# Silu MLP on one core: the last output group in row halves instead of whole rows

## The chip, the core and the metric

The kernel runs on one core of a Trainium2 chip. The metric is device time in microseconds (us) for one launch. Engines are named as the profile names them: PE is TensorE (PEld its weight loads), ACT is ScalarE, DVE is VectorE, POOL is GpSimd, and SP is SyncE, which here only starts DMAs. SPq and ACTq are the DMA issues of SP and of ACT.

## The reference

```python
def reference(x, w1, w2):
    h = jnp.einsum("bsd,df->bsf", x, w1)
    h = _silu(h)
    out = jnp.einsum("bsf,fd->bsd", h, w2)
    return out
```

All arrays are bfloat16: x is 1 x 2048 x 640 (2048 tokens), w1 is 640 x 1728, w2 is 1728 x 640 and the output is 1 x 2048 x 640.

## The kernel before

The tokens are cut into four chunks of 512 (`NSC`). The hidden dimension of 1728 is 13 tiles of 128 (`FT`) and a rest of 64 (`FL`). The output dimension of 640 is split in columns 0 to 511 (`DA`) and 512 to 639.

The first matmul produces h transposed, hidden rows on partitions, with ScalarE's silu writing it to `hT` (and the rest of 64 rows to `hTt`, two chunks sharing its 128 partitions). The second matmul then has two forms. `Wide(c)` computes columns 512 to 639 for a chunk, transposed, and a DMA transpose turns them into `o_sb`. `Tok(st, a, e)` computes columns a to e of the 128 tokens of block `st`, with `hT` as the stationary operand and `w2s` as the moving one, into one PSUM bank of 512 fp32 columns.

Most of the second matmul is in groups of four units (`quad`). In it each 128-row step is cut in two halves of 64 rows. `half` issues one such matmul; two units in two banks are interleaved by `lanes`, one of them on rows 0 to 63 and the other on rows 64 to 127, so that two half matmuls can run at the same time. `begin` issues a unit's 13 halves on one side and the tail, which is the rest of 64 hidden rows; `rest` issues the 13 halves on the other side. A unit's first phase and its second phase write the same bank from different rows, so `rest` is preceded by a wait for the end of the first phase (`halfway`).

The last group is written out differently: five units, A, B and C of 512 columns and the fourth token block as E of 384 and G2 of 128 columns. The five tails come first, then each unit's 13 matmuls over whole rows of 128 (`whole`), unit by unit.

`close` casts a unit from PSUM to `o_sb` (`evac`, line 254 on DVE or 256 on ACT) and issues a store (line 88). A store through SP carries the columns 512 to 639 along when the unit ends at column 512, so that a row has 640 columns. Only G2's store goes through ACT's DMA queue. The order on each engine is the order in the program. At the end SP waits for all of its stores and ACT for its own.

Every matmul of this stage has the profile line 175 (`mm`) and every load or store the line 88 (`load`), so groups are told apart by operands and time.

Of the kernel before, what the change touches and what calls it, by code (L numbers as in the profile page):

```python
# [9 lines left out]
def bass_standalone__dense_activation_silu__prompt_kernel(  # L10
# [10 lines left out]
    of = out.flatten_outer_dims()  # L21
    S, D = xf.shape
    F = w1.shape[1]
    P = 128
# [3 lines left out]
    FT = F // P  # L28
    FL = F - FT * P
# [4 lines left out]
    DA = 512  # L34
# [4 lines left out]
    pe, act, dve, pool, sp = nc.tensor, nc.scalar, nc.vector, nc.gpsimd, nc.sync  # L39

    with ExitStack() as es:
        def sb(name, shape, dtype):
            return es.enter_context(nc.sbuf_tensor(name, shape, dtype))
# [3 lines left out]
        w2s = sb("w2s", [P, FT, D], bf16)  # L47
        w2t = sb("w2t", [P, D], bf16)
        hT = sb("hT", [P, FT, S], bf16)
        hTt = sb("hTt", [P, NSC // 2, SCH], bf16)  # L50
        oT = sb("oT", [P, S], bf16)
        o_sb = sb("o_sb", [P, S // P, D], bf16)
        warm = sb("warm", [P, 32], fp32)
        z = sb("z", [P, HB], bf16)
        ps = es.enter_context(nc.psum_tensor("ps", [P, NB, BANK], fp32))
# [4 lines left out]
        def sem(name):  # L60
            s = es.enter_context(nc.semaphore(name))
            count[s.name if hasattr(s, "name") else name] = 0
            return [s, 0]

        def tick(ins, s, n=1):
            ins.then_inc(s[0], n)
            s[1] += n
            return (s, s[1])

        def wait(eng, *points):  # L70
            for pt in points:
                if pt is None:
                    continue
                s, v = pt
                key = (id(eng), id(s))
                if seen.get(key, 0) < v:
                    eng.wait_ge(s[0], v)
                    seen[key] = v

        s_pe, s_act, s_dve = sem("s_pe"), sem("s_act"), sem("s_dve")  # L80
# [4 lines left out]
        def load(eng, out_ap, in_ap):  # L85
            s = sem(f"s_ld{n_dma[0]}")
            n_dma[0] += 1
            return tick(eng.dma_start(out=out_ap, in_=in_ap), s, 16)
# [85 lines left out]
        def mm(o, l, r, start, stop, shared=False):  # L174
            return pe.matmul(o, lhsT=l, rhs=r, start=start, stop=stop, skip_group_check=shared)  # L175
# [7 lines left out]
        def step(b, k, ft, c0, c1, start=False, stop=False):  # L183
            for h0 in (0, HC):
                ins = mm(ps[h0:h0 + HC, b, :], w1s[:, k, ft * P + h0:ft * P + h0 + HC],
                         xT[:, k, c0:c1], start, stop, shared=True)
            return ins

        def part(k, ft, c0, c1, start=False, stop=False):
            return step(ft, k, ft, c0, c1, start, stop)  # L190
# [18 lines left out]
        for ft in range(NO):  # L209
            t = tick(part(4, ft, 0, SCH, stop=True), s_pe)  # L210
# [11 lines left out]
        for ft in range(NO, FT):  # L222
# [3 lines left out]
            for k in range(DT):  # L226
                ins = step(b, k, ft, 0, SCH, start=(k == 0), stop=(k == DT - 1))
            silu(hT[:, ft, 0:SCH], ps[:, b, :], b, tick(ins, s_pe))
        for c in range(1, NSC):
            wait(pe, ld_xc[c])  # L230
            for ft in range(FT):
                b = bank()
                for k in range(DT):
                    ins = step(b, k, ft, c * SCH, (c + 1) * SCH, start=(k == 0), stop=(k == DT - 1))
                h_last = silu(hT[:, ft, c * SCH:(c + 1) * SCH], ps[:, b, :], b, tick(ins, s_pe))
        h_tail = []
        for q in range(NSC // 2):
            b = bank()
            for k in range(DT):
                for hh in range(2):  # L240
                    c = 2 * q + hh
                    ins = mm(ps[hh * FL:(hh + 1) * FL, b, :], w1s[:, k, F0:F],
                             xT[:, k, c * SCH:(c + 1) * SCH],
                             start=(k == 0), stop=(k == DT - 1), shared=True)
# [4 lines left out]
        def evac(out_ap, in_ap, b, after, eng=None):  # L249
            e = eng or (dve, act)[evac_n[0] % 2]  # L250
            evac_n[0] += 1
            wait(e, after)
            if e is dve:
                r = tick(dve.tensor_copy(out=out_ap, in_=in_ap), s_dve)  # L254
            else:
                r = tick(act.copy(out=out_ap, in_=in_ap), s_act)  # L256
            bank_free[b] = r
            return r

        JB = SCH // P  # L260
        HP = P // 2
        stores, stores_a = [], []
        s_turn = [sem(f"s_turn{c}") for c in range(NSC)]
        st_w = [None] * NSC

        class Wide:
# [11 lines left out]
            def tail(self):  # L278
                q, r0 = self.c // 2, (self.c % 2) * FL
                return mm(ps[:, self.b, :], w2t[r0:r0 + FL, DA:D], hTt[r0:r0 + FL, q, :],  # L280
                          False, False, shared=True)

            def close(self, t):
                c = self.c
                r = evac(oT[:, c * SCH:(c + 1) * SCH], ps[:, self.b, :], self.b, t)
                wait(sp, r)
                st_w[c] = tick(sp.dma_start_transpose(
                    out=o_sb[:, c * JB:(c + 1) * JB, DA:D],
                    in_=oT[:, c * SCH:(c + 1) * SCH],
                ), s_turn[c], 16)  # L290

        class Tok:
# [8 lines left out]
                return mm(ps[:, self.b, 0:self.e - self.a], hT[r0:r0 + HP, ft, st * P:(st + 1) * P],  # L301
                          w2s[r0:r0 + HP, ft, self.a:self.e], start, stop, shared=True)

            def whole(self, ft, stop):
                st = self.st
                return mm(ps[:, self.b, 0:self.e - self.a], hT[:, ft, st * P:(st + 1) * P],
                          w2s[:, ft, self.a:self.e], False, stop, shared=True)

            def tail(self, start=False):
                st = self.st  # L310
                c = st // JB
                q, r0, col = c // 2, (c % 2) * FL, (st % JB) * P
                return mm(ps[:, self.b, 0:self.e - self.a], hTt[r0:r0 + FL, q, col:col + P],
                          w2t[r0:r0 + FL, self.a:self.e], start, False, shared=True)

            def close(self, t, eng=None):
                st, a, e = self.st, self.a, self.e
                r = evac(o_sb[:, st, a:e], ps[:, self.b, 0:e - a], self.b, t, eng)
                last = a > 0
                if e == DA and not last:  # L320
                    e = D
                q = act if last else sp
                wait(q, r, st_w[st // JB])
                (stores_a if last else stores).append(
                    load(q, of[st * P:(st + 1) * P, a:e], o_sb[:, st, a:e]))

        def lanes(up, down):
            for i in range(max(len(up), len(down))):
                for lane in (up, down):
                    if i < len(lane):  # L330
                        lane[i]()

        def begin(u, r0):
            def end():
                wait(pe, *h_tail)
                u.halfway = tick(u.tail(), s_pe)
            return [lambda ft=ft: u.half(r0, ft, ft == 0, False) for ft in range(FT)] + [end]

        def rest(u, r0, done):
            ops = [lambda ft=ft: u.half(r0, ft, False, ft == FT - 1) for ft in range(FT - 1)]  # L340
            ops.append(lambda: done.append(tick(u.half(r0, FT - 1, False, True), s_pe)))
            return ops
# [18 lines left out]
        last = None  # L361
        for q in range(NSC // 2):
            for j in range(0, JB, 2):
                s0, s1 = 2 * q * JB + j, (2 * q + 1) * JB + j
                if q < NSC // 2 - 1 or j < JB - 2:
                    quad(Tok(s0), Tok(s1), Tok(s0 + 1), Tok(s1 + 1))
                else:
                    last = (s0, s1)
        s0, s1 = last
        A, B, C, E, G2 = Tok(s0), Tok(s1), Tok(s0 + 1), Tok(s1 + 1, 0, 384), Tok(s1 + 1, 384, DA)  # L370
        wait(sp, st_w[(s1 + 1) // JB])
        stores.append(load(sp, of[(s1 + 1) * P:(s1 + 2) * P, DA:D], o_sb[:, s1 + 1, DA:D]))
        for u in (A, B, C, E, G2):
            u.open()
        wait(pe, *h_tail)
        for u in (A, B, C, E, G2):
            u.tail(start=True)
        for u, eng in ((A, dve), (B, act), (C, act), (E, dve), (G2, act)):
            for ft in range(FT):
                ins = u.whole(ft, ft == FT - 1)  # L380
            u.close(tick(ins, s_pe), eng)
        wait(sp, *stores)
        wait(act, *stores_a)

# [27 lines left out]
```

## Time and profile before

| | us |
|---|---|
| Median of 3 runs | 124.34 (124.25 to 124.39) |
| Profiled execution | 124.57 |
| Its span | 123.1 |
| PE busy | 120.7 (98%) |
| ACT busy | 38.8 (32%) |
| DVE busy | 6.9 (6%) |
| Last quad and the last group, until the last cast starts | 98.0 to 121.27 |
| From the last cast to the span's end | 1.8 |

The granted TensorE clock is full (1.0) from 5 us to the last matmul. Matmul records overlap: the duration of one (for example 0.376 us for 64 rows by 512 columns) includes the latency through the array, and the rate is read from the distance between starts. A DMA issue on SPq or ACTq is the time for which the issuing engine is occupied; the landing of the data comes later (a median of 1.8 us from issue for SP's output stores of 160 KB). A few matmul records may be missing.

### The profile page before, as it was taken

Reading aid. Unit: us, or ns where it says so; the run is one execution under the profiler, and the core shown is the slowest. Engines: PE = TensorE matmul, PEld = TensorE weight load, DVE = VectorE, ACT = ScalarE, POOL = GpSimd, SP = SyncE. Lnnn points to the kernel's source line nnn. Section 1 sums busy time; section 2 is a strip of 40 time slices with the busy share of each in tenths; the row PEclk is TensorE's granted clock in tenths of the full one; section 3 lists DMA queues with packets and bytes.
Section 4 is the critical chain, followed back from the end, with each engine's and each line's share of the span. In section 5 each row is a group of like instructions: output and inputs, shape, how many; then the busy total and the mean of one; then the engine's idle time right before and its main releaser. Section 6 shows DMA issues by size and latency. Waiting matters only on the chain.

```text
span 123.1 us, 2300 instructions
## 1 busy us (share of the span) xinstructions
PE 120.7 (98%) x1056; PEld 59.5 (48%) x1057; DVE 6.9 (6%) x11; ACT 38.8 (32%) x67; POOL 0.3 (0%) x5
## 2 busy tenths in 40 slices
PE   8999999999999999999999999999999999999993
PEld 5455555555555555555544444444444444444452
DVE  0000000000000000000000022002201300222001
ACT  4002975555555555555530011001101200110110
POOL 0000000000000000000000000000000000000000
PEclk9999999999999999999999999999999999999999
DMA  6999935555992000000000004202200220023112
GB/s 146 263 248 315 135 86 108 104 87 92 280 392 77 0 0 0 8 0 0 0 0 5 0 12 113 51 0 107 107 0 5 107 107 0 5 107 117 53 67 83
DMA packets 19625, 10.42 MB, mean 85 GB/s; under 512 B 13728, under 2 KB 19104, under 8 KB 19616
## 3 DMA queue, kind: packets, MB, share of 16 engines
q1 hardware_dynamic: 19328, 10.08, 31.0%
q10 hardware_dynamic: 288, 0.20, 0.6%
q8 instruction: 8, 0.13, 0.5%
q14 instruction: 1, 0.01, 0.0%
HBM read 4.51 MB, written 2.62 MB: 58 GB/s over the span
## 4 chain that ended last, share of the span: by engine, by line
PE 98%; issue 0%; ACT 0%; DVEq 0%
PE ps L175 95%; PE ps L132 3%; ACT o_sb L256 0%; DVEq L397 0%
## 5 line engine op out<-in xcount | busy, mean ns | idle before, releaser
L175 PE MATMUL ps<-xT,w1s 128*64 128x512 bf16 x540 | 59.2, 382 | 0.0
L175 PE MATMUL ps<-w2s,hT 64*128 64x512 bf16 (+3 forms) x376 | 46.0, 369 | 0.2 <-issue 0.2
L175 PEld LDWEIGHTS ps<-xT,w1s 128*64 128x64 bf16 x540 | 30.6, 111 | 28.3 <-issue 0.9
L179 ACT ACTIVATE hT<-ps 128x512 bf16<-128x512 f32 x52 | 30.0, 608 | 29.2 <-PE ps L175 29.2
L175 PEld LDWEIGHTS ps<-w2s,hT 64*128 64x128 bf16 (+1 forms) x377 | 21.0, 95 | 24.1 <-issue 0.2
L256 ACT CAST o_sb<-ps 128x512 bf16<-128x512 f32 (+1 forms) x9 | 4.9, 550 | 41.5 <-PE ps L175 41.5
L175 PE MATMUL ps<-hT,w2s 64*128 64x512 bf16 x104 | 11.7, 376 | 0.0
L175 PEld LDWEIGHTS ps<-hT,w2s 64*128 64x128 bf16 x104 | 5.0, 94 | 6.3 <-issue 0.4
L254 DVE CAST o_sb<-ps 128x512 bf16<-128x512 f32 (+1 forms) x8 | 5.4, 675 | 40.5 <-PE ps L175 40.5
L254 DVE CAST oT<-ps 128x512 bf16<-128x512 f32 x2 | 1.4, 691 | 73.5 <-PE ps L175 73.5
L256 ACT CAST oT<-ps 128x512 bf16<-128x512 f32 x2 | 1.2, 585 | 10.6 <-PE ps L175 10.6
L132 PE MATMUL ps<-z 128*128 128x256 bf16 (+1 forms) x15 | 3.3, 419 | 0.4 <-DVE z L125 0.4
L175 PE MATMUL ps<-w2t,hTt 64*128 64x512 bf16 (+2 forms) x17 | 2.9, 363 | 0.0
L132 PEld LDWEIGHTS ps<-z 128*128 128x128 bf16 (+1 forms) x15 | 1.9, 143 | 1.5 <-issue 0.4
L179 ACT ACTIVATE hTt<-ps 128x512 bf16<-128x512 f32 x2 | 1.2, 597 | 1.0 <-PE ps L175 1.0
L144 ACT ACT_TABLE_LOAD x1 | 1.3, 1283 | 0.5 <-issue 0.5
L175 PEld LDWEIGHTS ps<-w2t,hTt 64*128 64x128 bf16 x17 | 0.9, 94 | 1.1
L175 PE MATMUL ps<-hTt,w2t 64*128 64x512 bf16 x4 | 0.8, 376 | 0.0
L175 PEld LDWEIGHTS ps<-hTt,w2t 64*128 64x128 bf16 x4 | 0.2, 94 | 0.2
L144 ACT ACTIVATE warm<-warm 128x32 f32<-128x32 f32 x1 | 0.2, 229 | 0.0
L125 DVE MEMSET z<- 128x128 uint32 x1 | 0.2, 165 | 0.2 <-issue 0.2
L140 POOL MEMSET warm<- 128x32 f32 x1 | 0.1, 124 | 0.0
(4 smaller groups left out, 0.4 us busy)
## 6 DMA issues: line engine op xcount, KB each, us to landing
out_dram<-o_sb SPq DMA_DIRECT2D x15, 160.0 KB, 1.8
w2s<-in_w_dram SPq DMA_DIRECT2D x1, 1120.0 KB, 6.6
w1s<-in_w_dram SPq DMA_DIRECT2D x4, 256.0 KB, 3.4
w2s<-in_w_dram SPq DMA_DIRECT2D x1, 960.0 KB, 8.6
w1s<-in_w_dram SPq DMA_DIRECT2D x1, 560.0 KB, 5.6
w1s<-in_w_dram SPq DMA_DIRECT2D x1, 320.0 KB, 4.4
xT<-in_x_dram SPq DMA_TRANSPOSE x18, 3.7
w1s<-in_w_dram ACTq DMA_DIRECT2D x1, 160.0 KB, 2.4
```

The costliest lines, as they stand in the source:

```text
L125: p_z = early(lambda: tick(dve.memset(z[:, :], 0.0), s_dve), ET.DVE, False)
L132: pe.matmul(ps[c0:c0 + w, 3, 0:HB], lhsT=z[:, 0:w], rhs=z[:, :], start=True, stop=True)
L140: p_warm = early(lambda: tick(pool.memset(warm[:, :], 0.0), s_pool), ET.Pool, False)
L144: act.activation(out=warm[:, :], in_=warm[:, :], func=ACT.Silu)
L175: return pe.matmul(o, lhsT=l, rhs=r, start=start, stop=stop, skip_group_check=shared)
L179: r = tick(act.activation(out=out_ap, in_=in_ap, func=ACT.Silu), s_act)
L254: r = tick(dve.tensor_copy(out=out_ap, in_=in_ap), s_dve)
L256: r = tick(act.copy(out=out_ap, in_=in_ap), s_act)
```

## The change

The last group keeps the scheme of the quads. The four last token blocks become three pairs: two whole blocks of 512 columns (`Tok(s0)`, `Tok(s1)`), the other two blocks' columns 0 to 383, and their columns 384 to 511. All three pairs run `begin`, then all three run `rest`. In each pair ACT casts the first unit and DVE the second. The stores of the first two pairs go through SP. Of the last pair, ACT's queue stores the first unit and SP the second. As two blocks are now split, SP stores the columns 512 to 639 of both of them on their own, ahead of the group (one block before). `whole` is gone, and `close` takes the queue as an argument.

```diff
-            def whole(self, ft, stop):
-                st = self.st
-                return mm(ps[:, self.b, 0:self.e - self.a], hT[:, ft, st * P:(st + 1) * P],
-                          w2s[:, ft, self.a:self.e], False, stop, shared=True)
-
-            def tail(self, start=False):
+            def tail(self):
...
-            def close(self, t, eng=None):
+            def close(self, t, eng=None, q=sp):
                 st, a, e = self.st, self.a, self.e
                 r = evac(o_sb[:, st, a:e], ps[:, self.b, 0:e - a], self.b, t, eng)
-                last = a > 0
-                if e == DA and not last:
+                if a == 0 and e == DA:
                     e = D
-                q = act if last else sp
                 wait(q, r, st_w[st // JB])
-                (stores_a if last else stores).append(
+                (stores_a if q is act else stores).append(
                     load(q, of[st * P:(st + 1) * P, a:e], o_sb[:, st, a:e]))
...
         s0, s1 = last
-        A, B, C, E, G2 = Tok(s0), Tok(s1), Tok(s0 + 1), Tok(s1 + 1, 0, 384), Tok(s1 + 1, 384, DA)
-        wait(sp, st_w[(s1 + 1) // JB])
-        stores.append(load(sp, of[(s1 + 1) * P:(s1 + 2) * P, DA:D], o_sb[:, s1 + 1, DA:D]))
-        for u in (A, B, C, E, G2):
-            u.open()
-        wait(pe, *h_tail)
-        for u in (A, B, C, E, G2):
-            u.tail(start=True)
-        for u, eng in ((A, dve), (B, act), (C, act), (E, dve), (G2, act)):
-            for ft in range(FT):
-                ins = u.whole(ft, ft == FT - 1)
-            u.close(tick(ins, s_pe), eng)
+        M = 384
+        wait(sp, st_w[s0 // JB], st_w[s1 // JB])
+        for st in (s0 + 1, s1 + 1):
+            stores.append(load(sp, of[st * P:(st + 1) * P, DA:D], o_sb[:, st, DA:D]))
+        pairs = [(Tok(s0), Tok(s1)), (Tok(s0 + 1, 0, M), Tok(s1 + 1, 0, M)),
+                 (Tok(s0 + 1, M, DA), Tok(s1 + 1, M, DA))]
+        for X, Y in pairs:
+            X.open()
+            Y.open()
+            lanes(begin(X, 0), begin(Y, HP))
+        for X, Y in pairs:
+            dx, dy = [], []
+            wait(pe, X.halfway, Y.halfway)
+            lanes(rest(Y, 0, dy), rest(X, HP, dx))
+            if X.a:
+                X.close(dx[0], act, act)
+                Y.close(dy[0], dve, sp)
+            else:
+                X.close(dx[0], act, sp)
+                Y.close(dy[0], dve, sp)
```

More of the change, by code (lines that the diff above doesn't have):

```diff
@@ L313, in tail @@
                 return mm(ps[:, self.b, 0:self.e - self.a], hTt[r0:r0 + FL, q, col:col + P],
-                          w2t[r0:r0 + FL, self.a:self.e], start, False, shared=True)
-            def close(self, t, eng=None):
+                          w2t[r0:r0 + FL, self.a:self.e], False, False, shared=True)
+            def close(self, t, eng=None, q=sp):
                 st, a, e = self.st, self.a, self.e
                 r = evac(o_sb[:, st, a:e], ps[:, self.b, 0:e - a], self.b, t, eng)
-                last = a > 0
-                if e == DA and not last:
+                if a == 0 and e == DA:
                     e = D
-                q = act if last else sp
                 wait(q, r, st_w[st // JB])
-                (stores_a if last else stores).append(
+                (stores_a if q is act else stores).append(
                     load(q, of[st * P:(st + 1) * P, a:e], o_sb[:, st, a:e]))
```

## The prediction

> **What bounds the kernel now.** I read the page first (busy shares and chain), then the groups with shapes kept apart, then the timeline of the last 20 us, then the timeline and landings of SP's DMAs there.
>
> ```profile
> PE 120.7 (98%) x1056; PEld 59.5 (48%) x1057; DVE 6.9 (6%) x11; ACT 38.8 (32%) x67; POOL 0.3 (0%) x5
> ...
> PE 98%; issue 0%; ACT 0%; DVEq 0%
> ```
>
> TensorE (PE) is the chain from start to end. The edit touches only what comes after 109.28 us, so that stage's rows decide: PE's last 12 us, then 1.8 us of cast, store and landing.
>
> ```profile
> 106.67 0.59 ACT L256 CAST o_sb<-ps 128x512 bf16<-128x512 f32 x1 [8.26 <-PE ps L175]
> ...
> 109.28 0.60 PE L175 MATMUL ps<-w2t,hTt 64*128 64x512 bf16 x5
> 109.47 0.58 ACT L256 CAST o_sb<-ps 128x512 bf16<-128x512 f32 x1 [2.22 <-PE ps L175]
> ...
> 109.80 11.26 PEld L175 LDWEIGHTS ps<-w2s,hT 128*128 128x128 bf16 x65 [0.21 <-issue]
> 110.03 11.20 PE L175 MATMUL ps<-w2s,hT 128*128 128x512 bf16 x64 [0.16 <-issue]
> 112.82 0.69 DVE L254 CAST o_sb<-ps 128x512 bf16<-128x512 f32 x1 [2.62 <-PE ps L175]
> 115.63 0.58 ACT L256 CAST o_sb<-ps 128x512 bf16<-128x512 f32 x1 [5.57 <-PE ps L175]
> 118.43 0.59 ACT L256 CAST o_sb<-ps 128x512 bf16<-128x512 f32 x1 [2.22 <-PE ps L175]
> 120.55 0.56 DVE L254 CAST o_sb<-ps 128x384 bf16<-128x384 f32 x1 [7.03 <-PE ps L175]
> 121.27 0.27 ACT L256 CAST o_sb<-ps 128x128 bf16<-128x128 f32 x1 [2.25 <-PE ps L175]
> 121.57 0.35 ACTq L88 DMA_DIRECT2D out_dram<-o_sb  x1
> ```
>
> Each cast starts when its unit's last matmul is done, so the distances between casts are what 13 matmul steps take. Row halves: 106.67 to 109.47, 2.80 us for 13 pairs. Whole rows: 2.81 and 2.80 us for 13 of 512 columns, 2.12 for 13 of 384, 0.72 for 13 of 128. By the matmuls' own starts, a step is 0.2158 us for a pair of halves or a whole of 512, 0.1625 for a whole of 384 and 0.0559 for a whole of 128. Two concurrent halves do the work of one whole in the same time.
>
> The idle 0.16 at 110.03 is not all real: 65 weight loads stand against 64 matmuls, and the 12 steps before the first unit's last matmul put its first at 109.81, where a record is missing. The preceding tails stop streaming at 109.71. Passing from half tiles to whole ones costs about 0.10 us.
>
> ```profile
> 110.22 0.33 SPq L88 DMA_DIRECT2D out_dram<-o_sb  x1
> ```
> ```profile
> 110.61 0.42 SPq L88 DMA_DIRECT2D out_dram<-o_sb  x1
> ```
> ```profile
> 111.08 0.46 SPq L88 DMA_DIRECT2D out_dram<-o_sb  x1
> ```
>
> These are three stores that SP issues back to back, each from its own narrow timeline. The first takes 0.33 us; the second, issued 0.05 after it, takes 0.42; the third 0.46. SP's other second-in-a-row stores show 0.37 to 0.43, its isolated ones 0.33. The length does not follow the bytes: 0.42 and 0.33 are 160 KB, 0.46 is 32 KB, and the isolated 96 KB store at 121.13 takes 0.33. So SP cannot send stores closer together than about 0.48 us.
>
> **The change, part by part.** All times count from the span's start. The profiled execution took 124.57 us, 1.48 more than its span of 123.09; the median of the runs is 124.34. I take the difference of the spans and add it to either.
>
> Matmuls. Before, from the slot at 109.275: tails 0.216 + 0.163 + 0.056, the passage of 0.10, 39 steps of 512 (8.42), 13 of 384 (2.11), 13 of 128 (0.73); the last matmul starts at 121.015. After: 27 pair steps at each width, 14 in the first phase (13 halves and the tail) and 13 in the second. First phases: 3.021 to 112.30, 2.275 to 114.57, 0.783 to 115.35. Second phases: 2.805 to 118.16, 2.113 to 120.27, 0.727 to 121.00, so the last pair starts at 120.943. That is 0.07 us earlier: the passage goes, and the half tails are paired either way. The step of a 384 or 128 pair is not in the trace. Below: no less than the whole of the same width, since each half streams the same columns. Above: two weight loads now have to fit in one step. At 384 there is room, as two loads fit in 0.2158 beside other halves. At 128 the bound is a doubled step, 0.112. I take 0.056, the whole's step, because the second half of every 512 pair starts 0.004 us after the first. Ends: 0 and 14 + 13 steps of 0.056.
>
> Dispatch. PE's instructions rise from 140 to 324 here (loads and matmuls). At 12.24 PE's sequencer passes a wait, and 40 instructions later, at 12.79, the next: 0.014 us each, just what the 128 pairs use up, and it starts them with a queue filled during the 512 and 384 steps. Cost nothing; without that queue still about nothing.
>
> New waits on PE. The second phases wait for the ends of their first phases, which lie at least 3 us back; the last quad does the same with no idle. Pair three opens banks that were emptied by casts at 106.7 to 107.4. Nothing waits.
>
> SP's extra small store of columns 512 to 639 is queued after the one at 111.08 and occupies about 0.5 us, until 112.05; SP's next work comes at 119. It is hidden by 7 us of idle queue. Pair one's two stores go out at 119.0 to 119.9, also clear.
>
> The end. Pair two's last step starts at 120.109. A 384 matmul reports done 0.34 after its start, and the partner 0.034 later. VectorE then starts Y's cast at 120.47 and takes 0.556 (row at 120.55): 121.03. ScalarE starts X's at 120.51; its length I put at 0.48, in line between 0.585 at 512 and 0.265 at 128: 120.98. SP now has two 96 KB stores: the first goes at 121.01 and takes 0.33, the second at 121.39 and takes 0.43, until 121.82. Pair three meanwhile is done at 121.18 and 121.21. Its casts are 0.265 on ScalarE and, by the line through 0.692 at 512 and 0.556 at 384, 0.284 on VectorE; both halves are in SBUF by 121.48. X goes through ScalarE's queue at 121.52 (before: 121.57), takes the same 1.48 us to land, and is down at 123.01.
>
> Y must go through SP, where it stands behind the two 384 stores. Its data are ready at 121.48; SP is free at 121.86. This 0.38 us wait is what takes the place of the saved 0.10. From issue to landing, the same 32 KB takes 1.48 us on ScalarE's queue alone and 1.62 us as the third in a row on SP (the row at 111.08). I take 1.62, the row in the same position: 123.48, plus 0.04 from the last landing to the span's end, as before, gives 123.52. With 1.48 it is 123.38.
>
> Sum: 123.52 - 123.09 = +0.43 us; by the nearer row +0.29. The profiled execution would take 125.00, the median 124.77.
>
> A rule speaks to this step. The Trainium skill, DMA: Bandwidth & Descriptors, section "Issuing engines are not separate DMA queues", says that issuing from several engines saves only the sequencer's time, usually small beside the DMA. By the rule's "usually small" the queueing would be nothing and rival one below would be the result; this trace does not agree, with 0.48 us per store against 1.48 to 1.62 to land.
>
> **Rivals.**
>
> One, not slower: SP's issue does not hold the last store back. Were two 384 stores issued in under 0.6 us rather than 0.81, Y would leave near 121.5, land with X at 123.01, and the span would be 123.05: -0.04 us, median 124.30. For it: the 384 rows carry fewer bytes. Against it: three rows in which length ignores bytes. Chance 0.13.
>
> Two, weight loads bound the 128 pairs. For it: two loads per step, where the trace shows only one load per 0.056. Against it: at 512 the two loads of a pair start 0.004 apart with the same length. At 0.112 a step, the first phase ends 0.78 later. The second phase takes 1.45, so Y is in SBUF at 122.95, after SP is free (122.64), and it leaves at 122.97 with a short issue, landing near 124.45: span 124.49, +1.40, median 125.7. At half that extra, 0.084, the first phase costs 0.39, while the second's 0.36 hides behind SP's wait: +0.82, median 125.2. Chance 0.17. The Trainium skill, TensorE: Matmul & The Clock Gate, section "Back-to-back issue gap", gives about 81 ns per matmul sustained at 128 columns; as an estimate, 14 steps longer by 25 ns would add 0.35 and give 125.1. The whole matmuls here run at 56 ns, so the trace does not agree, and no run here shows it for halves.
>
> Three, the two queues share the path that spaces stores 0.48 apart. Then X's issue on ScalarE at 121.52 slips between SP's second and third, and Y leaves about 0.46 later: +0.89, median 125.2. For it: ScalarE's issue of 0.35 came 0.10 after SP's had ended, and exceeds SP's isolated 0.33. Against it: at 0.12 us ScalarE issued a load in 0.38 while SP was inside an issue of 1.33. Chance 0.10.
>
> That the kernel would not do what it says is out: its instruction order has the pairs and the four end stores as described.
>
> **How the numbers follow.** The forecast has 0.60, its own range 124.60 to 124.85. About 0.2% (0.25 us, 124.09 to 124.59) is what a measurement of this kernel can tell from no change. Slower: 0.55 of the forecast, 0.17 and 0.10 of rivals two and three, 0.82. Same: 0.05 of the forecast and 0.09 of rival one, 0.14. Faster: the remaining 0.04 of rival one, for a passage that cost more than 0.10. Range 124.40 to 125.30: it leaves out most of rival one (0.11) and the dear half of rival two (0.09).
>
> **What would show it.** Right: no idle between the last quad and pair one; casts of pair two near 120.5 and of pair three near 121.2; three SP issues from about 121.0, 121.4 and 121.86; the last landing is SP's small store, about 0.4 us after ScalarE's. The forecast is wrong if pair three's first phase takes over 0.9 us, if SP's third issue starts before 121.6, or if ScalarE's last issue lasts over 0.4 us.

## The result: 1.0034 times the time before

The changed kernel took 124.98 us in the median of 22 runs, the kernel before 124.52 us in 22 runs beside it: a ratio of 1.0034, with a 95% interval of 1.0019 to 1.0049. By the ratio that is +0.42 us, with 0.24 to 0.61 inside the interval (the two medians lie 0.46 apart). The prediction's sum was +0.43. It stood on a median of 124.34 from three runs, hence its 124.77; with the base at 124.52 the measured 124.98 lies above the 124.60 to 124.85 that it gave the forecast alone, while the difference is the one forecast. A second comparison gave 1.0028 (1.0005 to 1.0050).

The profiled execution after took 125.53 us with a span of 124.20, 1.12 more than before. Most of that is not the change. Executions of one kernel differ by about 1 us (1.5 us from the fastest to the slowest of the 22 before, 0.9 after), and in the profiles this lies in the opening: the first silu starts at 11.60 before and 12.29 after, but at 11.95 and 11.90 in second profiles of the two. From the first silu to the start of ScalarE's last cast of the last quad every profile of this case takes the same 97.87 us. So I set a mark at that cast, at 109.47 before and 110.16 after, which takes off 0.68. From there to the span's end is what this text calls the group's time: 13.615 us before, 14.047 after, **+0.432**. This part hardly varies. Second profiles gave 13.614 and 14.050, a third of the changed kernel 14.051.

First the timeline of ScalarE and VectorE in the last 15 us of the changed kernel (start, duration, engine, instruction):

```profile
110.16 0.58 ACT L256 CAST o_sb<-ps 128x512 bf16<-128x512 f32 x1 [2.22 <-PE ps L175]
...
119.04 0.69 DVE L254 CAST o_sb<-ps 128x512 bf16<-128x512 f32 x1 [8.16 <-PE ps L175]
119.07 0.58 ACT L256 CAST o_sb<-ps 128x512 bf16<-128x512 f32 x1 [8.33 <-PE ps L175]
121.15 0.56 DVE L254 CAST o_sb<-ps 128x384 bf16<-128x384 f32 x1 [1.42 <-PE ps L175]
121.19 0.48 ACT L256 CAST o_sb<-ps 128x384 bf16<-128x384 f32 x1 [1.53 <-PE ps L175]
121.88 0.29 DVE L254 CAST o_sb<-ps 128x128 bf16<-128x128 f32 x1 [0.17 <-PE ps L175]
121.91 0.27 ACT L256 CAST o_sb<-ps 128x128 bf16<-128x128 f32 x1 [0.25 <-PE ps L175]
122.21 0.35 ACTq L88 DMA_DIRECT2D out_dram<-o_sb  x1
```

The casts now come in pairs 0.03 us apart. The pair of 128 ends 0.73 us after the pair of 384. ScalarE's last cast starts 11.757 us after the mark, before it was 11.799: PE is a little earlier, as forecast.

Then PE's own rows in the first phase:

```profile
112.98 2.27 PE L175 MATMUL ps<-w2s,hT 64*128 64x384 bf16 x26
...
115.09 0.33 PE L175 MATMUL ps<-w2t,hTt 64*128 64x384 bf16 x2
...
115.26 0.89 PE L175 MATMUL ps<-w2s,hT 64*128 64x128 bf16 x26
...
115.98 0.22 PE L175 MATMUL ps<-w2t,hTt 64*128 64x128 bf16 x2
```

From 112.98 to 115.09 are 13 pair steps of 384 columns, 0.1625 us each; from 115.26 to 115.98 are 13 of 128, 0.0558 each. They are the steps of whole rows.

Last, SP's three final stores, each from a narrow timeline, of which the last row holds two issues (the second and the third, 122.07 to 122.98):

```profile
121.69 0.33 SPq L88 DMA_DIRECT2D out_dram<-o_sb  x1
```
```profile
122.07 0.43 SPq L88 DMA_DIRECT2D out_dram<-o_sb  x1
```
```profile
122.07 0.91 SPq L88 DMA_DIRECT2D out_dram<-o_sb  x2
```

The third store starts at 122.55, 0.38 us after its VectorE cast ended at 122.17. And the time to land of the two small stores at the end, in us from the start of their issue; first the one of the kernel before, then the two of the changed kernel:

```profile
out_dram<-o_sb ACTq DMA_DIRECT2D x1, 32.0 KB, 1.5
```
```profile
out_dram<-o_sb ACTq DMA_DIRECT2D x1, 32.0 KB, 1.7
out_dram<-o_sb SPq DMA_DIRECT2D x1, 32.0 KB, 1.6
```

ScalarE's store is issued first and down at 123.94, SP's at 124.16; the span ends 0.04 later.

### The profile page after: what moved, and what is told of

It reads as the page before. It is cut to its first block, busy times and chain, and to the rows that moved or that the text cites. A ratio compares the mean times of both kernels' runs of the same rounds, so it can differ in the third digit from the quotient of the medians.

```text
span 124.2 us, 2493 instructions
## 1 busy us (share of the span) xinstructions
PE 121.4 (98%) x1149; PEld 59.9 (48%) x1149; DVE 7.2 (6%) x12; ACT 38.7 (31%) x67; POOL 0.3 (0%) x5
## 4 chain that ended last, share of the span: by engine, by line
PE 95%; DMA 3%; ACT 0%; issue 0%
PE ps L175 95%; DMA xT<-in_x_dram 3%; ACT o_sb L256 0%
## 5 line engine op out<-in xcount | busy, mean ns | idle before, releaser
L175 PE MATMUL ps<-w2s,hT 64*128 64x512 bf16 (+2 forms) x468 | 46.5, 352 | 0.0
L175 PEld LDWEIGHTS ps<-w2s,hT 64*128 64x128 bf16 x468 | 21.8, 94 | 23.5
L256 ACT CAST o_sb<-ps 128x512 bf16<-128x512 f32 (+2 forms) x9 | 4.8, 538 | 41.6 <-PE ps L175 41.6
L254 DVE CAST o_sb<-ps 128x512 bf16<-128x512 f32 (+2 forms) x9 | 5.7, 632 | 40.6 <-PE ps L175 40.6
```

## The experiments

My theory was the prediction's: the two units of a pair end together, so their stores collide on SP, and the last store waits for its turn. The rivals left were that the paired matmuls themselves cost, that the number of stores at the end costs, or that the two queues share the path that spaces stores. In the table the issue is in us after the mark, the time to land runs from the start of the issue, and "end" is the group's time. In the text starts below 20 are counted from the mark, too, and those above 100 are a view's own times. e1 and e11 leave out stores, so part of their output is not written; e6 and e11 were run once, for the profile.

| kernel | last store to land: queue, issue | time to land | end |
|---|---|---|---|
| before | ScalarE, 12.09 | 1.48 | 13.615 |
| after | SP, 12.39 | 1.61 | 14.047 |
| e1, no 384 stores | ScalarE, 12.05 | 1.61 | 13.705 |
| e2, one 384 store on ScalarE | ScalarE, 12.24 | 1.76 | 14.060 |
| e5, merged stores | ScalarE, 12.09 | 1.71 | 13.838 |
| e9, whole rows | SP, 12.15 | 1.48 | 13.677 |
| e4, split 256 | ScalarE, 12.16 | 1.77 | 13.966 |
| e8, split 448 | SP, 12.79 | 1.58 | 14.412 |
| e11, e2 without the other 384 store | ScalarE, 12.23 | 1.46 | 13.738 |

**e1: take away the two stores ahead of the last one.** In `close`:

```diff
...
+                if a == 0 and e == M:
+                    return
                 wait(q, r, st_w[st // JB])
```

> The changed kernel without the two SP stores of columns 0 to 383 of the last two token blocks: those parts of the output are not written, all matmuls and casts stay. Measure: the group's time, from the start of ScalarE's last cast of the last quad to the span's end (before 13.62 us, after 14.05). Theory (the last store queues behind the two 384 stores on SP): it leaves when its cast ends, about 0.38 us earlier, and the group takes 13.58 to 13.70, 0.35 to 0.47 less than the changed kernel; ScalarE's store lands after about 1.48 us again instead of 1.73. Rival (the paired matmuls, or two small stores at once, are what costs): 13.9 to 14.05.

Measured: 13.705, which is 0.342 less than the changed kernel (ratio to before 0.9985, 0.9963 to 1.0006). The last two stores leave together:

```profile
121.03 0.33 SPq L88 DMA_DIRECT2D out_dram<-o_sb  x1
121.03 0.37 ACTq L88 DMA_DIRECT2D out_dram<-o_sb  x1
```

SP's store starts at 12.04 instead of 12.39, takes 0.33 instead of 0.43, and is down at 13.50, 0.50 earlier: the queue was what held it back. (This run takes away the two stores' bytes together with their turns; e2, e4 and e5 keep the bytes.) The gain stopped just short of what I expected, because the end passed to ScalarE's store, which landed in 1.61, not 1.48. PE's matmuls are the same as in the changed kernel, so the paired matmuls are not what costs.

**e9: undo the pairing, keep the units, casts and stores.** `whole` and the `start` of `tail` come back from the kernel before (not shown).

```diff
...
-            lanes(begin(X, 0), begin(Y, HP))
+        wait(pe, *h_tail)
+        for X, Y in pairs:
+            X.tail(True)
+            Y.tail(True)
         for X, Y in pairs:
             dx, dy = [], []
-            wait(pe, X.halfway, Y.halfway)
-            lanes(rest(Y, 0, dy), rest(X, HP, dx))
+            for u, d in ((X, dx), (Y, dy)):
+                for ft in range(FT):
+                    ins = u.whole(ft, ft == FT - 1)
+                d.append(tick(ins, s_pe))
```

> The units, casts and stores of the changed kernel, but with the matmuls over whole rows, one unit after the other (tails first, as in the kernel before). Theory (the two units of a pair end together, and that is what makes the stores collide): the units end 2.1 and 0.7 us apart, no store queues, and the group takes 13.62 to 13.72 us, 0.02 to 0.1 more than before. Rival (the larger number of stores at the end costs in itself): 14.0. The matmuls must show again the 0.10 us between tails and whole rows.

Measured: 13.677, and 13.679 in a second profile. The stores are the same in number and size as in the changed kernel, and 0.37 of the 0.43 us are gone:

```profile
119.76 0.56 DVE L254 CAST o_sb<-ps 128x384 bf16<-128x384 f32 x1 [3.53 <-PE ps L175]
120.49 0.27 ACT L256 CAST o_sb<-ps 128x128 bf16<-128x128 f32 x1 [2.36 <-PE ps L175]
120.78 0.34 ACTq L88 DMA_DIRECT2D out_dram<-o_sb  x1
121.21 0.29 DVE L254 CAST o_sb<-ps 128x128 bf16<-128x128 f32 x1 [0.89 <-PE ps L175]
```

Each unit ends at its own time, SP's last three stores start over 1 us apart, and the last of them leaves 0.03 after its cast:

```profile
121.53 0.33 SPq L88 DMA_DIRECT2D out_dram<-o_sb  x1
```

What remains against the kernel before (0.06) is 0.03 on PE, which has 13 more steps for the same columns (last matmul 11.576 against 11.543), and the longer last cast on VectorE (0.292 against 0.265). So the end times of the units make the cost, and the number of stores does not.

Its timed ratio was 0.9979 (0.9958 to 0.9999), faster than the groups allow. I timed it again beside the changed kernel.

> The whole-row kernel a second time. Its group took 13.68 us, 0.06 more than before, but its timed ratio was 0.9979 (0.9958 to 0.9999). If the group decides and the rest of that ratio was the spread between executions, which lies ahead of the group: group 13.66 to 13.69 again, ratio 0.999 to 1.002. If something in this kernel shortens the stages ahead of the group: again below 0.999, with the last quad's last ScalarE cast starting earlier than in the kernel before run beside it.

> The changed kernel, unchanged, timed again beside the whole-row kernel on one chip. Theory: 14.05 us for the group, ratio 1.0034 by the groups' difference of 0.43 us (1.0015 to 1.005 with the spread of such a measurement), and above the whole-row kernel, whose group is 0.37 us shorter.

Measured: 0.9994 (0.9974 to 1.0013) for whole rows and 1.0028 (1.0005 to 1.0050) for the changed kernel, groups of 13.679 and 14.051. From the first silu to the mark the whole-row kernel takes the usual 97.87 us, so nothing shows that its first ratio was more than the spread.

**e8 and e4: move the split.** `M = 448` and `M = 256` in place of 384.

> The changed kernel with M = 448: pairs of 512, 448 and 64 columns. Theory (SP's queue): the third pair ends sooner after the second, so the last SP store waits longer; its issue starts about 12.78 us into the group if a pair of 64 columns takes 0.03 us a step, and the group takes 14.35 to 14.50 us, 0.3 to 0.45 more than with 384. If loads or dispatch bound such a short pair at 0.056 us a step, 14.7 to 14.85, with the steps showing it. Rival (it is the bytes of the last stores that count, now smaller): below 14.05.

Measured with 448: 14.412, ratio 1.0058 (1.0030 to 1.0085). SP's third issue started at 12.79 (expected 12.78):

```profile
122.20 1.30 SPq L88 DMA_DIRECT2D out_dram<-o_sb  x3
122.32 0.35 ACTq L88 DMA_DIRECT2D out_dram<-o_sb  x1
```

The last store is half as large and the time is longer: it is the turn that counts, not the bytes. The rows of PE show that pairs of 64 columns keep pace:

```profile
115.74 0.54 PE L175 MATMUL ps<-w2s,hT 64*128 64x64 bf16 x26
...
116.12 0.19 PE L175 MATMUL ps<-w2t,hTt 64*128 64x64 bf16 x2
```

13 steps from 115.74 to 116.12, 0.029 us each, with two weight loads in every step.

> The changed kernel with M = 256: pairs of 512, 256 and 256 columns. Measured as the group's time (before 13.62 us, after 14.05). Theory (SP's queue): the second pair ends 1.42 us before the third, its two stores are issued by 11.7 us into the group, and the last SP store leaves when its cast ends, about 12.18; but the last casts take 0.37 and 0.43 us instead of 0.27 and 0.29, and two stores of 64 KB land together, in 1.6 to 1.7 us: 13.78 to 13.92. Rival (the number of stores at the end costs, wherever they stand): 14.05 or more.

Measured with 256: 13.966, ratio 1.0035 (1.0009 to 1.0060). SP's last store does leave when its cast is done, 12.175, and nothing is queued. But the end lies between my range and the rival's, 0.05 above mine: ScalarE's 64 KB store, issued 0.02 before SP's, took 1.77 to land, where I had allowed 1.7. Nothing waits for its turn here, and still 0.35 us are lost against the kernel before: ScalarE's last cast starts 0.04 earlier, is 0.11 longer (0.372 against 0.265), and its store takes 0.29 longer to land.

**e2: send one of the two 384 stores through ScalarE's queue.**

```diff
-                X.close(dx[0], act, sp)
+                X.close(dx[0], act, act if X.e == M else sp)
```

> The changed kernel with the first of the two 384-column stores issued by ScalarE instead of SP. Theory (each issue occupies its engine): SP's last store goes out about 0.35 us earlier, but ScalarE's issue of 0.33 us now stands ahead of its own cast of the last unit, which starts about 0.13 us later, and its last store with it, so the group takes 13.78 to 13.92 us, about half of the loss given back. Rival (all stores are spaced 0.48 us whatever the queue): 14.05 or more. Second rival (an issue on ScalarE does not hold back its casts): 13.6 to 13.7.

Measured: 14.060, ratio 1.0018 (0.9996 to 1.0040). The end gained nothing, 0.14 above my range; that was the number of the first rival, but not for its reason. The issues are not spaced: two stores start 0.04 apart, and SP's last store starts at 12.04, 0.35 earlier than in the changed kernel.

```profile
121.11 0.37 ACTq L88 DMA_DIRECT2D out_dram<-o_sb  x1
121.15 0.83 SPq L88 DMA_DIRECT2D out_dram<-o_sb  x2
121.81 0.34 ACTq L88 DMA_DIRECT2D out_dram<-o_sb  x1
```

SP's last store comes down 0.19 us earlier than in the changed kernel, since 0.16 of the 0.35 goes back to a longer landing. The end has passed to ScalarE's last store. ScalarE's issue held its own next cast back by 0.19 us (start at 11.948 instead of 11.757; I had expected 0.13), so that store leaves 0.19 later than in the changed kernel, and it takes 1.76 to land (1.73 there, 1.48 in the kernel before).

All landings are longer: 1.90 and 2.02 for the 96 KB stores (1.60 and 1.71 in the changed kernel), 1.77 and 1.76 for the small ones. The windows view of this kernel, where the last two columns are the share of the DMA engines' time and GB/s, shows the engines full for 0.8 us (shares above 1 mean that packets overlap in the records):

```profile
122.00:122.40 0.40, 0.00 (x0) 0.00 (x0) 0.00 (x0) 0.00 (x0) 0.00 (x0) 1.00 0.97 334
122.40:122.80 0.40, 0.00 (x0) 0.00 (x0) 0.00 (x0) 0.00 (x0) 0.00 (x0) 1.00 1.11 289
```

In the changed kernel the same 256 KB keep them at 0.71, 0.83 and 0.66 over three such stretches. The late landing of ScalarE's small store could come from the other stores or from its place behind another on ScalarE's queue. To tell these apart I removed the other 384 store (on top of the edit above):

```diff
+                if a == 0 and e == 384 and q is sp:
+                    return
                 wait(q, r, st_w[st // JB])
```

> The kernel with the first 384-column store on ScalarE's queue (its group took 14.06 us), without the second 384-column store, whose part of the output is not written. There, both 384 stores were issued side by side, the DMA engines' busy share was full for 0.8 us, and the last 32 KB store landed 1.76 us after its issue, against 1.48 in the kernel before. Theory (stores side by side lengthen each other's landing on the DMA engines): without the second the last ScalarE store, still issued about 12.24 us into the group, lands in 1.48 to 1.62 us, and the group takes 13.77 to 13.90. Rival (the landing is longer because ScalarE issued two stores in a row): 14.0 or more.

Measured: 13.738. The last ScalarE store is issued at 12.23 and lands in 1.46, as fast as anywhere, although it is again ScalarE's second store in a row. In e2 the landing was longer because of the other 384 store, whose data the DMA engines move at the same time, and not because of ScalarE's queue. The end came 0.03 under my range.

**e5: one store for each pair**, 256 rows in one DMA; the small one on ScalarE's queue, waiting for both casts.

```diff
...
+                wait(q, rx, ry, st_w[s0 // JB], st_w[s1 // JB])
+                (stores_a if a else stores).append(
+                    load(q, of2[:, X.st:Y.st + 1:Y.st - X.st, a:e],
+                         o_sb[:, X.st:Y.st + 1:Y.st - X.st, a:e]))
```

> The changed kernel with one SP store for both 384-column parts and one store on ScalarE's queue for both 128-column parts (each waits for both casts). Theory: with one issue for each pair nothing queues; the last issue starts about 121.5 in the time of the kernel before and the group takes 13.55 to 13.75 us, equal to the kernel before within 0.1 us, as the 0.07 us saved on PE and the longer landing of a store twice as large nearly cancel. Rival (an issue's length grows with the rows it stores, 256 instead of 128): 13.8 to 14.0.

Measured: 13.838, ratio 1.0008 (0.9989 to 1.0027). Half of the loss is back. The end is 0.09 above my range. The last issue starts at 12.09, the same as in the kernel before, and an issue of 256 rows takes 0.38 to 0.40 us, barely more than one of 128 rows after a pause (0.33 to 0.35): the rival's reason falls, though its number came out. What is lost is in the last landing, 1.71 for 64 KB against 1.48 for 32 KB before. The 192 KB of the store ahead were still under way when it was issued (they are down at 13.57), which by e11 is the likely reason; no run here parts it from the doubled size.

**e6: five passages instead of one.** In the kernel before, each tail moves to just ahead of its unit:

```diff
-        for u in (A, B, C, E, G2):
-            u.tail(start=True)
         for u, eng in ((A, dve), (B, act), (C, act), (E, dve), (G2, act)):
+            u.tail(start=True)
             for ft in range(FT):
```

> The kernel before with each of the last group's five tails issued just ahead of its own unit, so that PE passes from half tiles to whole ones five times instead of once, and four times back. Price of a passage from half to whole by the trace of before: 0.10 us, to be seen five times. The tails no longer pair, which costs 0.43 us more of streaming. Theory (a passage costs 0.1 us in either direction): the last matmul starts 1.2 to 1.4 us later than before, and the group takes 14.8 to 15.0. If only the way to whole tiles costs, 0.8 us later: 14.4 to 14.5.

Measured: last matmul 1.27 us later, group 14.881, both as the theory had it.

```profile
113.00 0.39 PE L175 MATMUL ps<-w2t,hTt 64*128 64x512 bf16 x1
...
113.32 2.98 PE L175 MATMUL ps<-w2s,hT 128*128 128x512 bf16 x13
...
116.23 0.39 PE L175 MATMUL ps<-w2t,hTt 64*128 64x512 bf16 x1
...
116.55 2.49 PEld L175 LDWEIGHTS ps<-w2s,hT 128*128 128x128 bf16 x13 [0.23 <-issue]
```

From tail to whole row 0.318 us pass instead of 0.216, and from the last whole row of 512 (its 13th step starts at 115.92) to the next tail 0.31: 0.10 us in either direction. Eight more passages and 0.43 of unpaired tails make 1.23 of the 1.27. So the saving on PE in the prediction, one passage of 0.10 less 0.03 for more steps (13 of 512 columns give way to 13 of 384 and 13 of 128), has the right price.

**Repeats.** How well the mark works rests on these two:

> The kernel before, unchanged, profiled a second time, to see how well the group's time repeats (from the start of ScalarE's last cast of the last quad to the span's end; 13.62 us the first time). If what follows that cast depends on the kernel alone: 13.59 to 13.64, whatever the span is. If the spread between executions (about 1 us) lies in this stage too: anything up to 0.3 us away.

> The changed kernel, unchanged, profiled a second time. The group took 14.05 us the first time: 14.02 to 14.07 if it repeats, with SP's last three issues again about 0.48 us apart and the last landing 1.58 to 1.62 us after its issue; further away if the first profile was a chance.

Measured: 13.614 and 14.050, with the mark at 109.81 and 109.77. SP's three issues started 0.377 and 0.479 apart, so the 0.48 that I expected for both holds for the second alone. The last landed in 1.616.

No kernel here beats the one before. The best complete one is e9: its group is 0.06 us longer, and its ratios were 0.9979 and 0.9994.

## Why the prediction was right, step by step

**Matmuls.** The steps of 384 and 128 pairs were not in the trace of before, and I took those of whole rows. Measured 0.1625 and 0.056; the last pair starts 11.473 after the mark, against 11.543 before: 0.070 saved, 0.07 forecast. The prediction's reasons (two loads fit in the 0.2158 us of a 512 pair, whose halves start 0.004 apart) did not settle whether two weight loads fit in 0.1625 or 0.056 us. The step was a choice, with a rival of 0.17 against it, and the runs bear it out. The dear bound, 0.112 a step, is out, and with it rival two: even at 64 columns a pair takes 0.029. The 81 ns that the Trainium skill gives in TensorE: Matmul & The Clock Gate, "Back-to-back issue gap", does not agree with these rows either.

**Dispatch, new waits on PE, SP's extra store.** All were put at nothing. In the chain of work that ended last PE is one piece without idle up to the last matmul (start, duration, what):

```profile
3.75 118.14 PE ps L175 x1089
```

SP's extra store is issued 1.36 us after the previous pair's first one, with 7 us of pause behind it.

**Casts.** Estimated 0.48 and 0.284, measured 0.478 and 0.291.

**SP's queue.** Forecast starts, moved by the 0.68 of the mark: 121.69, 122.07, 122.54. Measured 121.69, 122.07, 122.55. The prediction's sentence that SP cannot send stores closer together than about 0.48 us is too wide: after a pause the second follows the first by 0.38 (110.22 and 110.61 in its own rows, 121.69 and 122.07 here), and only the third follows the second by 0.47 to 0.48. Its sum used the right distances. The rule on issuing from several engines (the Trainium skill, DMA: Bandwidth & Descriptors, "Issuing engines are not separate DMA queues") has two halves. That the time saved is "usually small" does not hold here: the last store stands in SP's queue for 0.38 us, against 1.61 to land. That all such DMAs share the same 16 DMA engines and interleave (the Trainium skill, the same section) agrees with e2, where a second queue saved SP's last store 0.35 us of waiting and 0.16 of it went back to a longer landing.

**Landing.** SP's last store took 1.61 of the 1.62 I had taken from the row in the same position. Why that row fits shows when the time is counted from the end of the issue: 1.18 here, 1.16 in that row, 1.13 for the last store of the kernel before. Most of the extra time is the issue itself, which is longer for a store that follows others at once (0.43 here and 0.46 in that row, against 0.35 on ScalarE before). The prediction did not say so. ScalarE's took 1.73, and I had carried 1.48 over from the kernel before, where it was alone. This term was mis-sized by 0.25 and cost the sum nothing, as SP's store ended 0.22 later still, where the prediction had 0.47. It matters for rival one: its -0.04 was too good. With SP's queue out of the way the group ends 0.09 after the kernel before (e1): 0.04 earlier at ScalarE's issue, 0.13 more to land.

**Rival three** falls as I had put it: ScalarE's issue of 0.35 (122.21 to 122.56) runs beside SP's second and into its third, and neither slips. Where both engines start an issue within 0.05 us of each other, ScalarE's takes 0.37 to 0.39 instead of 0.34 to 0.35 (e1, e2, e4). So what the queues share lies almost wholly behind the issue.

So the account along the last store to land is: -0.08 up to the start of its cast, 0.07 of it on PE; +0.03 for the longer cast, now on VectorE (0.291 against 0.265); +0.35 of waiting from the cast's end to the start of the issue (0.375 against 0.030); and +0.13 from there to the landing, of which 0.08 is the longer issue and 0.05 what follows it. This sums to 0.43. The wait and the longer issue, 0.42 together, both come of standing behind two others on SP: without them (e1) the same store leaves 0.03 after its cast with an issue of 0.33. That run gives back only 0.34, because ScalarE's store then ends the kernel.

## What to carry to other kernels

In this kernel the last 1.8 us belong to the last cast and its store, so look at when units end before making them end faster. Units that ended one after the other spread their stores by themselves; making them end in pairs saved 0.07 us on PE and lost several times that at the queue. When stores do collide, price the turn on the issuing queue, the landing beside other stores, and what else the other engine has to do: in e2 moving a store to ScalarE's queue removed the first only, and held back ScalarE's own last cast.

## What the runs showed that I had not expected

The time from issue to landing of the same 32 KB store on ScalarE's queue depends on its company: 1.46 to 1.48 us when SP's last store was issued over 0.4 us earlier (before, e9), 1.46 also when another of its size starts 0.19 earlier on SP (e11), but 1.61 when that one starts 0.01 earlier (e1), 1.73 just behind two of 96 KB on SP (after), 1.76 after two of these side by side (e2).

An issue of 256 rows is only about 0.05 us longer than one of 128 (e5), so one larger store takes a turn off the queue almost for free, though its data then move as one block.

Row-half pairs of 64 columns run at 0.029 us a step, two loads and two matmuls in each (e8). Passing between half tiles and whole rows costs 0.10 us either way (e6).
